# Retention and two dense layers on one core: retention units from the fifth on taken in pairs, the carried-state products in column halves

## The chip, the cores and the metric

The kernel runs on one core of a Trainium2 chip, as one program. The metric is the device time of an execution in microseconds. The engines are named as the profile names them: PE is TensorE (matmuls; its weight loads are listed as PEld), DVE is VectorE, ACT is ScalarE, POOL is GpSimd, SP is SyncE, which here issues nearly all transfers.

## What is computed

Retention over 2 batches, 8 heads, 768 tokens and a head dimension of 64, and after it two dense layers (512 to 1536, gated, back to 512; then 512 to 2048, leaky, back to 512). The change lies wholly in the retention.

```python
for t in range(S):
    state = gamma[None, :, None, None] * state + np.einsum('bhd,bhe->bhde', k[:, :, t], v[:, :, t])
    y[:, :, t] = scale * np.einsum('bhd,bhde->bhe', q[:, :, t], state)
...
a = x @ w_a
b = x @ w_b
return (a * b @ w_out).astype(np.float32)
...
g = np.maximum(0.01 * h, h)
return (g @ w_out).astype(np.float32)
```

## The kernel before

The 1536 tokens are three tiles of 512 (`t`), the 8 heads four pairs (`p`). A **unit** is one tile of one pair; there are 12, numbered 0 to 11, tile by tile. A unit's 512 tokens are four chunks of 128. The recurrence is rewritten by chunks: what a token gets from its own chunk is a masked product of scores, and what it gets from earlier chunks comes through a carried state of 64x64 for each head.

For each unit there are four loads of 256 KB (`q`, `k`, `n`, `v`: the queries and keys with the head dimension on the partitions, the keys and values with the tokens there), and then:

- `prep`: ACT scales `n` into `kd` in two instructions, and POOL scales `q` into `qs` (DVE does it for units 0 and 1).
- `scores`: PE multiplies `k` by `qs`, eight matmuls, for each head on its own 64 rows of the array; DVE scales and masks the two results into `P` (two instructions).
- `states`: PE multiplies `kd` by `v`, six or eight matmuls, each on 64 columns of the array; DVE runs the carried state along (`cr`, three or four short instructions).
- `spreads`: ACT copies the states into `wk`, a 128x128 matrix for each chunk, which has one head's state in each of two opposite corners and zeros elsewhere (four copies in units 4 to 7, two in the others).
- `within`: PE multiplies `v` by `P`, eight matmuls on 64 columns each, into a PSUM bank `xp`.
- `across`: PE adds `wk` times `qs` to the same bank, one matmul of 128 columns for each chunk that has a predecessor (three in units 0 to 7, four in units 8 to 11). Then `split` writes the result as a rounded part on ACT (`x4h` for unit 4) and the remainder on DVE (`x4l`).

A matmul in full precision shows as two matmul records and two weight loads. PSUM has eight banks, which are used in turn; a unit takes four (two for scores, one each for `kv` and `xp`).

Each engine works off its instructions in the order in which the program emits them. The order is written out by hand in the loop at the end of the attention part: in step `u`, scores and states of unit `u + 1`, then within and across of unit `u`, spreads of `u + 1`, `prep` of `u + 3`. Beside that, from step 3 on, each step takes one piece of preparing the first layer's first weight, `a0`: two ACT operations that take its 64-bit raw form apart (L255, L256), four on DVE (`sign` L270, min L272, shift L274, add L278), and a split into `a0h` (ACT) and `a0l` (DVE). The first matmuls of the first layer (`pa`, lines 215 to 217) use `a0h` twice and then `a0l`. The raw form of `a0`, 512 KB, is loaded ahead of unit 5's four loads.

Of the kernel before, what the change touches and what calls it, by code (L numbers as in the profile page):

```python
# [19 lines left out]
B, H, S, D = 2, 8, 768, 64  # L20
# [5 lines left out]
CPT = TT // P  # L26
# [4 lines left out]
NSLOT = 81  # L31
NRAW = 4
NEXTRA = 10
EARLY = 3
NWARM = 7
COUNT = {"a": FF1, "b": FF1, "wo": FF1, "wi": FF2, "wq": FF2}
HALF = FF2 // 2
# [150 lines left out]
def retention_moe_kernel(ctx: ExitStack, tc: tile.TileContext, ins, out):  # L188
    nc = tc.nc
# [46 lines left out]
    def load_weights():  # L236
        if at["load"] < len(order) and at["load"] < at["round"] + NRAW:
            kind, f = order[at["load"]]
            src, i = source[kind]
            t = rawp.tile([P, TT], I64, tag="raw", name=f"raw_{kind}{f}")  # L240
            nc.sync.dma_start(t, src[f, i])
            raws[kind, f] = t
            at["load"] += 1
# [128 lines left out]
    consts, chain, spread = [], [], []  # L372

    def attention_constants():
        for p in range(NPAIR):
            consts.append(ap.tile([P, P], F32, tag=f"cst{p}", name=f"cst{p}"))

        for p in range(NPAIR):
            chain.append([ap.tile([P, CPT, D], F32, tag=f"cr{p}{j}", name=f"cr{p}{j}") for j in range(2)])

        for i in range(2):
            spread.append(ap.tile([P, CPT, P], F32, tag=f"wk{i}", name=f"wk{i}"))
            nc.gpsimd.memset(spread[i][0:D, :, D:P], 0.0)
            nc.gpsimd.memset(spread[i][D:P, :, 0:D], 0.0)

    units = [(t, p) for t in range(NTILE) for p in range(NPAIR)]
    un = {}
# [95 lines left out]
    def spreads(u):  # L483

        if u >= len(units):
            return
        t, p = units[u]
        chunks = [t * CPT + j for j in range(CPT)]
        own = chain[p][t % 2]
        used = [c % CPB != 0 for c in chunks] + [False]  # L490
        runs = [(a, used.index(False, a)) for a in range(CPT) if used[a] and not (a and used[a - 1])]
        for a, b in runs:
            for h in range(2):
                r = slice(h * D, (h + 1) * D)
                nc.scalar.copy(spread[u % 2][r, a:b, h * D:(h + 1) * D], own[r, a:b])
        un[u]["S"] = spread[u % 2]

    cols = [slice(j * P, (j + 1) * P) for j in range(CPT)]

# [14 lines left out]
    def across(u):  # L514
        t, p = units[u]
        d = un.pop(u)
        xp = d["x"]
        later = [(t * CPT + j) % CPB != 0 for j in range(CPT)]
        for j, c in enumerate(cols):
            if later[j]:  # L520
                nc.tensor.matmul(xp[:, c], d["S"][:, j], d["qs"][:, c], start=False, stop=j == CPT - 1)  # L521
        x[t, p] = split(xp, f"x{u}")
        slots.done(4)


    h = {}
# [83 lines left out]
    for _ in range(NWARM):  # L610
        nc.tensor.matmul(wps, warm[:, 0:P], warm, start=True, stop=True)
    for u in range(1, 7):
        if u == 5:
            load_weights()
        loads(u)
    prep(0)
    def first_weights():
# [5 lines left out]

    micro = first_weights()
    prep(1)
    for u in range(-1, len(units)):
        scores(u + 1)
        slots.tick()
        if u == 0:
            within(u)  # L630
        states(u + 1)
        slots.tick()
        if u >= EARLY:
            next(micro, None)
        if u + 1 == len(units) - 1:
            spreads(u + 1)
        if u > 0:
            within(u)
        if u >= 0:
            across(u)  # L640
        if u + 1 < len(units) - 1:
            spreads(u + 1)
        if u < 0:
            prep(2)
        else:
            prep(u + 3)
        loads(u + 8)
        if u + 8 >= len(units) - 1:
            load_weights()
        slots.tick()  # L650
    att.close()
# [79 lines left out]
    for n in range(FF1 - 1, len(z.plan) - 2):  # L731
# [6 lines left out]
        name, j = z.plan[n]  # L738
# [109 lines left out]
    for n in range(FF2 - 1, len(z.plan) - 2):  # L848
# [7 lines left out]
        name, j = z.plan[n]  # L856
# [71 lines left out]
```

## Time and profile before

| | |
|---|---|
| runs | 588.07, 588.76, 588.95 us; median 588.76 us |
| span of the profiled execution, first to last instruction | 587.1 us |
| its own time | not told apart from the runs; the median lies 1.7 us above its span |
| PE busy | 578.6 us, 99% of the span |
| DVE busy | 452.5 us, 77% |
| ACT busy | 308.5 us, 53% |
| attention part | from the first scores at 6.31 us to the first matmul of the first layer at 50.27 us |

The page's shares are over the whole span. In the first twelfth of it, where the change is, the engines stand differently, so views of that stretch are used: the timeline (each instruction's start and length, merged where like ones follow each other), the windows (busy time in stretches) and the chain of waits. The idle time that a row of the timeline gives in brackets is the time in which the engine did nothing just before, and what ended it.

### The profile page before, as it was taken

What the parts mean: (1) busy time and instruction counts of PE and PEld (TensorE: products, weight loads), DVE (VectorE), ACT (ScalarE), POOL (GpSimd) and SP (SyncE); (2) the same over time, 40 slices, a digit from 0 to 9 for tenths busy, and PEclk for the clock granted to TensorE, in tenths of its full rate; (3) what the DMA queues carried; (4) which work ended last, traced back from release to release, by engine and by line L of the source; (5) the groups of instructions that cost most, each with busy time, mean ns of one, the idle gap of its engine ahead of it and who ended that gap; (6) DMA issues with size and microseconds to landing.
All of it is one profiled execution on the core that took longest, in us unless ns stands there. A gap on an engine that the chain in (4) does not pass through costs nothing.

```text
span 587.1 us, 8742 instructions
## 1 busy us (share of the span) xinstructions
PE 578.6 (99%) x3247; PEld 488.8 (83%) x3247; DVE 452.5 (77%) x937; ACT 308.5 (53%) x656; POOL 22.0 (4%) x32
## 2 busy tenths in 40 slices
PE   7999999999999999999999999999999999999997
PEld 5788788888888888888888888888888888888886
DVE  4795688889877788889999938657775766879992
ACT  4674446455354344547657356554633356788710
POOL 2430000000000000000000000000000000000000
PEclk9999999999999999999999999999999999999999
DMA  8991244555433343340014102213220000010111
GB/s 306 361 387 47 88 139 151 178 180 179 162 106 124 98 156 116 118 158 22 1 54 143 56 3 105 97 48 107 73 71 2 2 0 1 0 56 1 54 55 54
DMA packets 23050, 59.62 MB, mean 102 GB/s; under 512 B 2784, under 2 KB 4448, under 8 KB 23008
## 3 DMA queue, kind: packets, MB, share of 16 engines
q1 hardware_dynamic: 21600, 55.13, 28.0%
q0 software_dynamic: 1120, 3.67, 1.6%
q8 instruction: 25, 0.41, 0.3%
q10 hardware_dynamic: 288, 0.27, 0.1%
q14 instruction: 17, 0.14, 0.1%
HBM read 52.24 MB, written 6.82 MB: 101 GB/s over the span
## 4 chain that ended last, share of the span: by engine, by line
PE 91%; DMA 4%; DVE 3%; ACT 1%; issue 0%; SPq 0%; DVEq 0%
PE blk L216 11%; PE blk L215 11%; PE blk L217 11%; PE h L215 7%; PE h L216 7%; PE h L217 7%; PE pa L215 5%; PE pa L216 5%; PE pa L217 5%; PE pb L217 5%; PE pb L216 5%; PE pb L215 5%; DMA v<-in_vn 2%; PE xp L521 1%; DMA n<-in_kn 1%; PE sc L437 1%
## 5 line engine op out<-in xcount | busy, mean ns | idle before, releaser
L216 PE MATMUL blk<-form,form 128*128 128x512 f32 (+1 forms) x224 | 75.7, 338 | 0.0
L215 PE MATMUL blk<-form,form 128*128 128x512 f32 (+1 forms) x224 | 75.5, 337 | 0.0
L217 PE MATMUL blk<-form,form 128*128 128x512 f32 (+1 forms) x224 | 75.3, 336 | 0.0
L543 ACT COPY h<-pa 128x512 f32<-128x512 f32 x33 | 19.5, 590 | 84.6 <-PE pa L217 84.6
L779 ACT ACTIVATE g<-h 128x512 f32<-128x512 f32 x48 | 28.6, 597 | 62.2 <-PE h L217 62.2
L138 DVE TENSOR_TENSOR form<-g,form 128x512 fp32r<-128x512 f32 x112 | 57.3, 553 | 2.4 <-ACT form L132 0.7
L216 PE MATMUL blk<-forma,forma 128*128 128x512 f32 (+1 forms) x168 | 57.0, 339 | 0.4 <-DVE forma L138 0.4
L132 ACT CAST form<-g 128x512 fp32r<-128x512 f32 x112 | 52.6, 514 | 8.4 <-DVE g L113 6.4
L215 PE MATMUL blk<-forma,forma 128*128 128x512 f32 (+1 forms) x168 | 56.6, 337 | 0.0
L217 PE MATMUL blk<-forma,forma 128*128 128x512 f32 (+1 forms) x168 | 56.5, 336 | 0.0
L138 DVE TENSOR_TENSOR form<-wq,form 128x256 fp32r<-128x256 f32 x56 | 23.6, 421 | 35.5 <-ACT form L132 35.4
L215 PEld LDWEIGHTS blk<-form,form 128*128 128x128 f32 x224 | 42.5, 190 | 5.5
L216 PEld LDWEIGHTS blk<-form,form 128*128 128x128 f32 x224 | 42.5, 190 | 5.0
L217 PEld LDWEIGHTS blk<-form,form 128*128 128x128 f32 x224 | 42.3, 189 | 4.7
L138 DVE TENSOR_TENSOR forma<-h,forma 128x512 fp32r<-128x512 f32 x84 | 43.1, 553 | 0.8
L132 ACT CAST forma<-h 128x512 fp32r<-128x512 f32 x84 | 38.8, 511 | 0.0
L216 PEld LDWEIGHTS blk<-forma,forma 128*128 128x128 f32 x168 | 31.8, 189 | 4.6 <-DVE forma L138 0.9
L215 PEld LDWEIGHTS blk<-forma,forma 128*128 128x128 f32 x168 | 31.8, 190 | 4.1
L217 PEld LDWEIGHTS blk<-forma,forma 128*128 128x128 f32 x168 | 31.7, 189 | 3.5
L113 DVE TENSOR_TENSOR g<-g,g 128x512 f32<-128x512 f32 (+1 forms) x56 | 30.7, 571 | 3.6 <-ACT g L779 3.6
L546 DVE TENSOR_TENSOR h<-h,pb 128x512 f32<-128x512 f32 x33 | 22.5, 683 | 8.4 <-PE pb L217 5.4
L132 ACT CAST forma<-wo 128x256 fp32r<-128x256 f32 x42 | 17.1, 407 | 17.4 <-PE blk L217 13.2
(3091 smaller groups left out, 1447.3 us busy)
## 6 DMA issues: line engine op xcount, KB each, us to landing
raw_wi<-in_w SPq DMA_DIRECT2D x16, 512.0 KB, 3.2
raw_wq<-in_w SPq DMA_DIRECT2D x16, 512.0 KB, 3.4
raw_a<-in_wab SPq DMA_DIRECT2D x12, 512.0 KB, 3.2
raw_b<-in_wab SPq DMA_DIRECT2D x12, 512.0 KB, 3.4
raw_wo<-in_wo SPq DMA_DIRECT2D x12, 512.0 KB, 3.3
q<-in_qT SPq DMA_DIRECT2D x12, 256.0 KB, 5.2
n<-in_kn SPq DMA_DIRECT2D x12, 256.0 KB, 5.2
v<-in_vn SPq DMA_DIRECT2D x12, 256.0 KB, 5.3
```

What stands on the lines that cost most here:

```text
L113: queue.append((cost, lambda piece=piece: run(*(self.A(*x[1:], j)[piece] for x in (d, x0, x1)))))
L132: nc.scalar.copy(h, src)
L138: nc.vector.tensor_sub(*todo.pop(0))
L215: nc.tensor.matmul(ps, w[0], x[0], start=first, stop=False, skip_group_check=more)
L216: nc.tensor.matmul(ps, w[0], x[1], start=False, stop=False, skip_group_check=more)
L217: nc.tensor.matmul(ps, w[1], x[0], start=False, stop=last, skip_group_check=more)
L437: nc.tensor.matmul(sc[h][:, c], d["k"][r, c], d["qs"][r, c], start=True, stop=True)
L521: nc.tensor.matmul(xp[:, c], d["S"][:, j], d["qs"][:, c], start=False, stop=j == CPT - 1)
L543: nc.scalar.copy(h[t, f], pa)
L546: nc.vector.tensor_mul(h[t, f], h[t, f], pb)
L779: nc.scalar.activation(g[t, f], ps, AF.Lrelu, alpha=0.01)
```

## The change

Units 0 to 3 keep their steps. From unit 4 on, two units make a group, and in each step a kind of work is done for both before the next kind: scores of both, states of both, within of both units of the group before, across of both. Further:

- In `across` each matmul of 128 columns becomes two of 64 columns, one for each head, which write to the two halves of the bank's partitions.
- `prep` of the next two units is emitted ahead of `across` (where the coming group is a pair), and so its `kd` stands ahead of the `x..h` of `split` in ACT's order.
- `spreads` of both units of a group follow each other; there are four `wk` matrices instead of two, so POOL clears two more at the start. In the last group they stand ahead of `across`, as before.
- The pieces of preparing `a0` come two at a time at the end of a step, first after the group of units 4 and 5, last after the group of units 8 and 9.
- The raw form of `a0` is loaded between unit 9's and unit 10's loads.

```diff
--- before.py
+++ after.py
@@ -31,7 +31,7 @@
 NSLOT = 81
 NRAW = 4
 NEXTRA = 10
-EARLY = 3
+SINGLE = 4
 NWARM = 7
 COUNT = {"a": FF1, "b": FF1, "wo": FF1, "wi": FF2, "wq": FF2}
 HALF = FF2 // 2
@@ -378,7 +378,7 @@
         for p in range(NPAIR):
             chain.append([ap.tile([P, CPT, D], F32, tag=f"cr{p}{j}", name=f"cr{p}{j}") for j in range(2)])
 
-        for i in range(2):
+        for i in range(4):
             spread.append(ap.tile([P, CPT, P], F32, tag=f"wk{i}", name=f"wk{i}"))
             nc.gpsimd.memset(spread[i][0:D, :, D:P], 0.0)
             nc.gpsimd.memset(spread[i][D:P, :, 0:D], 0.0)
@@ -492,8 +492,8 @@
         for a, b in runs:
             for h in range(2):
                 r = slice(h * D, (h + 1) * D)
-                nc.scalar.copy(spread[u % 2][r, a:b, h * D:(h + 1) * D], own[r, a:b])
-        un[u]["S"] = spread[u % 2]
+                nc.scalar.copy(spread[u % 4][r, a:b, h * D:(h + 1) * D], own[r, a:b])
+        un[u]["S"] = spread[u % 4]
 
     cols = [slice(j * P, (j + 1) * P) for j in range(CPT)]
 
@@ -518,7 +518,11 @@
         later = [(t * CPT + j) % CPB != 0 for j in range(CPT)]
         for j, c in enumerate(cols):
             if later[j]:
-                nc.tensor.matmul(xp[:, c], d["S"][:, j], d["qs"][:, c], start=False, stop=j == CPT - 1)
+                for h in range(2):
+                    r = slice(h * D, (h + 1) * D)
+                    nc.tensor.matmul(
+                        xp[r, c], d["S"][:, j, r], d["qs"][:, c], start=False, stop=j == CPT - 1
+                    )
         x[t, p] = split(xp, f"x{u}")
         slots.done(4)
 
@@ -610,8 +614,6 @@
     for _ in range(NWARM):
         nc.tensor.matmul(wps, warm[:, 0:P], warm, start=True, stop=True)
     for u in range(1, 7):
-        if u == 5:
-            load_weights()
         loads(u)
     prep(0)
     def first_weights():
@@ -623,29 +625,46 @@
 
     micro = first_weights()
     prep(1)
-    for u in range(-1, len(units)):
-        scores(u + 1)
+    groups = [[u] for u in range(SINGLE)] + [[u, u + 1] for u in range(SINGLE, len(units), 2)]
+    prepared = 2
+    for n in range(-1, len(groups)):
+        now = groups[n] if n >= 0 else []
+        then = groups[n + 1] if n + 1 < len(groups) else []
+        for u in then:
+            scores(u)
         slots.tick()
-        if u == 0:
-            within(u)
-        states(u + 1)
+        if n == 0:
+            within(0)
+        for u in then:
+            states(u)
         slots.tick()
-        if u >= EARLY:
+        if n > 0:
+            for u in now:
+                within(u)
+        last = n + 2 == len(groups)
+        if last:
+            for u in then:
+                spreads(u)
+        if len(then) == 2:
+            while prepared <= then[-1] + 2:
+                prep(prepared)
+                prepared += 1
+        for u in now:
+            across(u)
+        if not last:
+            for u in then:
+                spreads(u)
+        while prepared <= (then or now)[-1] + 2:
+            prep(prepared)
+            prepared += 1
+        if now and now[0] >= SINGLE:
             next(micro, None)
-        if u + 1 == len(units) - 1:
-            spreads(u + 1)
-        if u > 0:
-            within(u)
-        if u >= 0:
-            across(u)
-        if u + 1 < len(units) - 1:
-            spreads(u + 1)
-        if u < 0:
-            prep(2)
-        else:
-            prep(u + 3)
-        loads(u + 8)
-        if u + 8 >= len(units) - 1:
+            next(micro, None)
+        for u in now:
+            loads(u + 7)
+            if u == 2:
+                load_weights()
+        if now and now[-1] + 7 >= len(units):
             load_weights()
         slots.tick()
     att.close()
```

**Order on ACT.** The first piece is ACT's order before, from the `kd` of unit 9 on (a number behind a name is the unit; `wk` is followed by the number of its buffer, `cr` by that of the head pair; `x2` stands for two instructions).

```order
L415 ACTIVATE kd9_98_608<-n9_59_333,small_74 128x4x64 x2
L209 CAST x7h_102_652<-xp7_640 128x512
L495 COPY wk0_88<-cr00_80 64x4x64 x2
L415 ACTIVATE kd10_104_658<-n10_69_391,small_74 128x4x64 x2
L209 CAST a0h_108_687<-a0_73_419 128x512
L209 CAST x8h_110_704<-xp8_691 128x512
L495 COPY wk1_91<-cr10_82 64x4x64 x2
L415 ACTIVATE kd11_112_710<-n11_80_452,small_74 128x4x64 x2
L209 CAST x9h_116_752<-xp9_739 128x512
```

The same place on ACT with the change, from the `kd` of unit 10 on.

```order
L415 ACTIVATE kd10_102_681<-n10_79_491,small_74 128x4x64 x2
L415 ACTIVATE kd11_104_686<-n11_96_609,small_74 128x4x64 x2
L209 CAST x6h_106_697<-xp6_663 128x512
L209 CAST x7h_108_707<-xp7_672 128x512
L495 COPY wk0_88<-cr00_80 64x4x64 x2
L495 COPY wk1_91<-cr10_82 64x4x64 x2
L495 COPY wk2_94<-cr20_84 64x4x64 x2
L495 COPY wk3_97<-cr30_86 64x4x64 x2
L209 CAST x8h_114_797<-xp8_767 128x512
L209 CAST x9h_116_809<-xp9_776 128x512
L209 CAST a0h_118_816<-a0_93_599 128x512
```

The `kd` of unit 11 stood behind `x8h`; now it stands ahead of `x6h`. The `a0h` stood ahead of `x8h`, and now stands behind the four spreads of units 8 to 11 and behind `x8h` and `x9h`.

**Order on DVE.** Before, from the add of `a0` (the ISA row) on.

```order
L278 ISA a0_73_419<-a0_73_419,low0_420 128x1024
L210 TENSOR_TENSOR x7l_103_653<-xp7_640,x7h_102_652 128x512
L443 SCALAR_TENSOR_TENSOR P90_106_673<-sc90_663,small_74,causal_75 128x512
L443 SCALAR_TENSOR_TENSOR P91_107_675<-sc91_664,small_74,causal_75 128x512
L478 SCALAR_TENSOR_TENSOR cr10_82<-cr10_82,small_74,kv9_677 128x64 x3
L210 TENSOR_TENSOR a0l_109_688<-a0_73_419,a0h_108_687 128x512
L210 TENSOR_TENSOR x8l_111_705<-xp8_691,x8h_110_704 128x512
```

With the change, from the remainder of unit 6 to that of `a0`.

```order
L210 TENSOR_TENSOR x6l_107_698<-xp6_663,x6h_106_697 128x512
L210 TENSOR_TENSOR x7l_109_708<-xp7_672,x7h_108_707 128x512
L272 TENSOR_SCALAR a0_93_599<-a0_93_599 128x512
L274 SCALAR_TENSOR_TENSOR a0_93_599<-a0_93_599,sign0_603 128x512
L443 SCALAR_TENSOR_TENSOR P100_110_729<-sc100_719,small_74,causal_75 128x512
L443 SCALAR_TENSOR_TENSOR P101_111_731<-sc101_720,small_74,causal_75 128x512
L443 SCALAR_TENSOR_TENSOR P110_112_743<-sc110_733,small_74,causal_75 128x512
L443 SCALAR_TENSOR_TENSOR P111_113_745<-sc111_734,small_74,causal_75 128x512
L478 SCALAR_TENSOR_TENSOR cr20_84<-cr20_84,small_74,kv10_747 128x64 x3
L478 SCALAR_TENSOR_TENSOR cr30_86<-cr30_86,small_74,kv11_757 128x64 x3
L210 TENSOR_TENSOR x8l_115_798<-xp8_767,x8h_114_797 128x512
L210 TENSOR_TENSOR x9l_117_810<-xp9_776,x9h_116_809 128x512
L278 ISA a0_93_599<-a0_93_599,low0_600 128x1024
L210 TENSOR_TENSOR a0l_119_817<-a0_93_599,a0h_118_816 128x512
```

The add of `a0` stood behind the states of unit 8, and now stands behind everything of units 8 to 11 but `x10l` and `x11l`; `a0l` follows it.

## Rows read from the trace of the kernel before

**Rows 1.** The page, busy us of each engine (share of the span) and instructions.

```profile
PE 578.6 (99%) x3247; PEld 488.8 (83%) x3247; DVE 452.5 (77%) x937; ACT 308.5 (53%) x656; POOL 22.0 (4%) x32
```

**Rows 2.** Windows: stretch, us, busy by engine, clock, DMA share, GB/s.

```profile
34.00:37.00 3.00, 3.00 (x49) 2.59 (x48) 2.96 (x8) 2.46 (x7) 0.40 (x2) 1.00 1.06 401
...
120.00:587.00 467.00, 463.57 (x2306) 393.38 (x2305) 362.35 (x754) 243.37 (x519) 5.96 (x11) 1.00 0.23 75
```

**Rows 3.** The chain of waits in order of time: start us, us, what.

```profile
16.13 7.49 DMA n<-in_kn
...
26.72 1.02 PE xp L521 x6
```

**Rows 4.** Timeline of PE: start us, us, engine, line, operation, shapes, count.

```profile
31.00 1.16 PE L437 MATMUL sc<-qs,k 64*128 64x128 f32 x16
...
32.49 1.04 PE L506 MATMUL xp<-P,v 128*64 128x128 f32 x16
33.47 0.94 PE L521 MATMUL xp<-qs,wk 128*128 128x128 f32 x6
34.34 1.16 PE L437 MATMUL sc<-qs,k 64*128 64x128 f32 x16
...
40.13 1.16 PE L521 MATMUL xp<-qs,wk 128*128 128x128 f32 x8
41.22 1.16 PE L437 MATMUL sc<-qs,k 64*128 64x128 f32 x16
...
50.81 0.40 PE L217 MATMUL pa<-x0h,a0l 128*128 128x512 f32 x1
```

**Rows 5.** Groups of 0 to 130 us: within's weight loads, busy us, mean ns, idle.

```profile
L506 PEld LDWEIGHTS xp<-P,v 128*64 128x64 f32 x192 | 10.5, 137 | 0.3
```

**Rows 6.** Timeline of DVE, 27 to 56 us.

```profile
31.76 0.42 DVE L272 TENSOR_SCALAR a<-a 128x512 f32<-128x512 f32 x1
...
34.65 0.68 DVE L274 SCALAR_TENSOR_TENSOR a<-a,sign 128x512 int32<-128x512 int32 x1
35.25 0.68 DVE L210 TENSOR_TENSOR x6l<-xp,x6h 128x512 fp32r<-128x512 f32 x1
35.85 1.40 DVE L443 SCALAR_TENSOR_TENSOR P<-sc,small,causal 128x512 f32<-128x512 f32 x2
37.17 0.90 DVE L478 SCALAR_TENSOR_TENSOR cr<-cr,small,kv 128x64 f32<-128x64 f32 x3
37.99 0.68 DVE L278 CUSTOM_DVE_ANT_0 a<-a,low 128x1024 uint16<-128x1024 uint16 x1
38.59 0.69 DVE L210 TENSOR_TENSOR x7l<-xp,x7h 128x512 fp32r<-128x512 f32 x1
...
41.33 0.69 DVE L210 TENSOR_TENSOR a0l<-a,a0h 128x512 fp32r<-128x512 f32 x1
```

**Rows 7.** Timeline of ACT, 22 to 56 us.

```profile
23.64 0.91 ACT L415 ACTIVATE kd<-n,small 128x256 f32<-128x256 f32 x2 [1.99 <-DMA n<-in_kn]
...
34.92 1.15 ACT L495 COPY wk<-cr 64x128 f32<-64x128 f32 x4
...
39.92 0.60 ACT L209 CAST a0h<-a 128x512 fp32r<-128x512 f32 x1
41.38 0.59 ACT L209 CAST x8h<-xp 128x512 fp32r<-128x512 f32 x1 [0.86 <-PE xp L521]
41.86 0.83 ACT L495 COPY wk<-cr 64x256 f32<-64x256 f32 x2
42.72 0.91 ACT L415 ACTIVATE kd<-n,small 128x256 f32<-128x256 f32 x2
```

**Rows 8.** Timeline of POOL: the scaling of q for units 4, 5, 9, 10, 11.

```profile
18.32 1.27 POOL L419 TENSOR_TENSOR qs<-q,cst 128x512 f32<-128x512 f32 x1 [2.82 <-DMA q<-in_qT]
22.36 1.27 POOL L419 TENSOR_TENSOR qs<-q,cst 128x512 f32<-128x512 f32 x1 [2.76 <-DMA q<-in_qT]
...
32.95 1.28 POOL L419 TENSOR_TENSOR qs<-q,cst 128x512 f32<-128x512 f32 x1 [1.39 <-DMA q<-in_qT]
36.83 1.28 POOL L419 TENSOR_TENSOR qs<-q,cst 128x512 f32<-128x512 f32 x1 [2.60 <-DMA q<-in_qT]
39.47 1.28 POOL L419 TENSOR_TENSOR qs<-q,cst 128x512 f32<-128x512 f32 x1 [1.35 <-PE kv L466]
```

## Prediction

> **What bounds the kernel now.** I read the page first: TensorE is busy 99% of the span [rows 1], and from 120 us on it is busy 463.6 of 467 us [rows 2]. So whatever delays or advances the first matmul of the first layer arrives at the end undiminished, and the question is only when that matmul can run. I then read the windows and timelines of the attention part. There the reader is to see three things that are all close to full. TensorE is busy 3.00 of 3.00 us between 34 and 37 us, but VectorE is at 2.96 [rows 2], and the transfers bring a unit (four loads) every 2.65 us: the scaling of q starts at 22.36 us for unit 5 and at 32.95 for unit 9, so 10.6 us for four [rows 8]. TensorE needs 3.33 us for a unit (31.00 to 34.34 [rows 4]). The chain of waits says the same in order of time: up to 26.7 us it runs through loads (a load of n is 7.49 us of it), after that through TensorE [rows 3]. So TensorE has only some 0.4 to 0.6 us in 3.3 to win before VectorE or the loads take over.
>
> **What the change takes off TensorE.** Eight matmul records of `across` go from 40.13 to the next scores at 41.22, 1.09 us; six go from 33.47 to 34.34, 0.87 [rows 4]. A matmul is two records, so a record costs 0.11, six should cost 0.66, and 0.21 is over. A unit in all: scores 8 x 0.11 (two rows of heads side by side), states 6 x 0.055, within 8 x 0.11, across 0.66, sum 2.75, against 3.33 measured. The 0.58 that is over falls on three changes between shapes (64 rows, 64 columns, whole array), 0.19 each. With column halves `across` has the shape of `within`, so one change goes in each of 12 units: 2.3 us. Pairs remove one of two others for every second unit, eight in four pairs: 1.5 us. One change appears, before the first layer: 0.2. Sum 3.6 us less work for TensorE. The halves themselves cost nothing if two heads' halves run side by side as those of `within` do: its 16 records take 0.98 us [rows 4].
>
> Here a rule speaks against the change. The row first: within's 192 loads of 64 columns last 137 ns each, 26.3 us added up, but together occupy 10.5 us with 0.3 us of idle before them [rows 5], so loads and matmuls of that very shape overlap. The Trainium skill, page "TensorE: Matmul & The Clock Gate", Part 3, states that a weight load overlaps matmuls in flight only when their row group differs, which two column halves over all 128 rows do not fulfil. By that sentence across would grow; by the row it does not. I take the row, and give the rule's mechanism as the last rival.
>
> **What the loads do.** The raw weight stood ahead of unit 5's loads: between units 4 and 5 lie 4.04 us (18.32 to 22.36) where 2.65 is usual [rows 8], so it costs 1.4. Units 5 to 9 now land 1.4 us sooner. Units 10 and 11 gain nothing, since the raw weight now stands ahead of them: q of unit 11 lands by 39.5 as before [rows 8], and its n two loads later, at 39.4 + 2 x 0.66 = 40.7. Issuing each unit's loads a step later, and SyncE's shorter path to units 5 to 9, change nothing else: SyncE is that far ahead. The two further clears on GpSimd run before its first operand lands. The two further `wk` buffers cost nothing.
>
> **What the pairs add: waits in ACT's order.** This is the term that decides. The `kd` of both coming units now stand ahead of the rounding of the finished units. So `x3h` waits for n of unit 7, `x4h` for n of unit 9, `x6h` for n of unit 11, and VectorE waits behind these. Before, `kd11` stood two units later, and nobody waited for it (it ran at 42.72, with no idle before it [rows 7]).
>
> I work the timetable out from row lengths, as distances from one start to the next. VectorE: `P` of a unit 1.32, states 0.82, `x..l` 0.60, shift 0.60, add 0.60, min 0.4 [rows 6]. ACT: `kd` 0.9, `x..h` 0.48, spreads 0.86, `a0h` 0.6 [rows 7]; 0.15 for handing over.
>
> TensorE first. Scores 5 now follow scores 4 directly; `qs5` is there at 22.36 - 1.4 + 1.28 = 22.3, while scores 4 end at 18.32 + 1.27 + 1.1 = 20.7: it stands 1.6. Scores 7 (q at 26.3, ready at 27.5) stand some 0.9, within 6 up to 0.9, because its bank is freed by `x4l`, which waits through `x4h` and `kd9` for n of unit 9 (32.9 to 34.1). Then `x6h`:
>
> - n of unit 11 lands at 40.7; `kd11` until 41.5, `x6h` until 42.0, VectorE starts `x6l` at 42.1. It was free by 41.5 even in the late case (34.1 + 0.9 + 0.48 + 0.15 = 35.6, then two remainders, sign, two `P` and two states, 1.2 + 0.5 + 2.64 + 1.64 = 6.0).
> - VectorE: `x6l`, `x7l` 1.2, min and shift 1.0, `P` of 10 and 11 2.64, states 1.64, sum 6.5: 48.6.
> - ACT: the spreads of unit 10 overlap the last states; those of unit 11 from 48.7 to 49.6, `x8h` until 50.05. TensorE gets `across` of 10 and 11 after its spreads, 48.7 + 2 x 0.9 = 50.5, about where it ended before in spite of 3.6 us less work.
> - VectorE: `x8l`, `x9l` 50.2 to 51.4, add 52.0; ACT `a0h` 52.1 to 52.75; `a0l` at 52.8, done at 53.4.
>
> Before, `a0l` ran at 41.33 [rows 6], nine microseconds ahead of need. The matmul that reads it ran at 50.81 [rows 4]; now it can't before 53.4. That is 2.6 us later. The next weights follow `x11l` on VectorE, which moves by about as much, so the distance between TensorE and VectorE is as before, and no later wait changes. The sum: the profiled execution has a span of 587.1 and the runs' median is 1.7 above it; span 589.7, time 588.76 + 2.6 = 591.4 us.
>
> Bounds of the sum. Handing over between engines is not in one row: 0.1 or 0.2 each, on about ten steps, gives half a microsecond either way. The price of a change between shapes doesn't enter, since TensorE waits at the end. A load held up: q of unit 10 came 3.88 us after unit 9's, not 2.65 [rows 8]; if that hold falls away the chain gains at most 0.6, as VectorE is busy until 41.5 otherwise. So 590.4 to 592.4 for this case.
>
> **Rivals.**
>
> *TensorE stays the bound* and the 3.6 us arrive: 585.2. For it: TensorE is continuously busy from 26.7 us on [rows 2, 3]. Against it: VectorE has 0.04 us in 3 left [rows 2]. It decides where n of units 7, 9 and 11 stands: this case needs each of them landed and scaled by the time that TensorE ends `across` of the group before (about 25.7, 32.5 and 39.3), and by the rows they land at 27.6, 32.9 to 34.1, and 40.7. Two would have to come over a microsecond sooner, without the raw weight being moved further. 9%.
>
> *The loads come sooner than reckoned*: with the raw weight out of the stream, the units behind it land more than 1.4 us earlier and unit 11 some 1.2 to 2 us earlier; then the whole timetable from scores 7 on moves by that much, less what VectorE can't follow, and 0.6 to 1.2 us of loss remain: about 589.7, no change that can be seen. For it: the interval before unit 10 holds 1.2 us that isn't bytes. Against it: what lies ahead of unit 11 in the queue is the same. 14%.
>
> *A second hold falls on units 10 and 11*: as the one of 1.2 us, added to the timetable: 592.6. 5%.
>
> *The halves don't run side by side*, so the change doesn't do what it says: each pair of halves then pays a load of 0.137 [rows 5] that nothing hides, 6 x 0.137 in eight units, 8 x 0.137 in four, 11 us; waits of some 5 us in the stage take up part, and 6 come on top of my sum: 597. That is what the skill's rule above would make of it. The row of the same shape speaks against it. 2%.
>
> **How the numbers follow.** My case has 70%. Slower by over 0.2% (1.2 us, about what a measurement of this kernel can tell from no change) are it, the second hold and the last rival: 0.77. Within it is the case of sooner loads: 0.14. Faster is TensorE as the bound: 0.09. My case and the second hold are 75%, so the range must reach down into the sooner loads: 589.0 to 592.8.
>
> **What would show it.** Right: in the timeline of ACT, `kd` of units 7, 9 and 11 with idle before them that a load of n ended, and `x3h`, `x4h`, `x6h` straight behind; TensorE idle some 1.6 us before the second scores of units 4 and 5; at the end of the attention part about 2 us of TensorE idle, ended by `a0h` or `a0l`; across as twelve records of 64 columns, two starting side by side, with 0.2 us less per unit, and TensorE's work in the stage shorter although the stage is longer. Wrong: if ACT never waits for n ahead of an `x..h`; if `a0l` runs before TensorE is through with across of unit 11; or if the delay at the first matmul of the first layer isn't found again at the end, because a later stage had slack.

## The result, and the profile after

The changed kernel took 591.80, 590.75, 591.70 and 591.97 us, median 591.75, beside 588.66 us for the kernel before on the same chip: ratio 1.0051, 95% interval 1.0037 to 1.0066, so 3 us slower. The profiled execution (591.80 us) has a span of 589.9 us against 587.1. The forecast was 591.4, slower. That it came so close is luck: two errors of 1.7 us each cancel, so the steps matter here more than the sum.

The busy times hardly differ from [rows 1], as the change only reorders. The page after:

```profile
PE 578.1 (98%) x3327; PEld 489.1 (83%) x3327; DVE 452.4 (77%) x937; ACT 308.3 (52%) x656; POOL 23.2 (4%) x36
```

The timeline of PE after, which answers to [rows 4]: start, length, shapes, records, and in brackets the idle time before and what ended it.

```profile
21.39 1.16 PE L437 MATMUL sc<-qs,k 64*128 64x128 f32 x16 [1.14 <-POOL qs L419]
...
26.79 1.16 PE L437 MATMUL sc<-qs,k 64*128 64x128 f32 x16 [0.77 <-POOL qs L419]
...
28.63 1.92 PE L506 MATMUL xp<-P,v 128*64 128x128 f32 x32
30.38 1.48 PE L523 MATMUL xp<-qs,wk 128*64 128x128 f32 x24
...
34.52 1.92 PE L506 MATMUL xp<-P,v 128*64 128x128 f32 x32
...
46.78 2.38 PE L523 MATMUL xp<-qs,wk 128*64 128x128 f32 x32
51.24 0.50 PE L215 MATMUL pa<-x0h,a0h 128*128 128x512 f32 x1 [2.08 <-ACT a0h L209]
51.58 0.39 PE L216 MATMUL pa<-x0l,a0h 128*128 128x512 f32 x1
51.97 0.79 PE L217 MATMUL pa<-x0h,a0l 128*128 128x512 f32 x1
52.56 0.63 PE L215 MATMUL pa<-x1h,a0h 128*128 128x512 f32 x1
52.99 0.63 PE L216 MATMUL pa<-x1l,a0h 128*128 128x512 f32 x1
...
61.38 0.39 PE L215 MATMUL pb<-x0h,b0h 128*128 128x512 f32 x1
```

The same matmuls of the first layer in the kernel before, and the first that uses the second matrix (`pb`):

```profile
51.05 0.40 PE L215 MATMUL pa<-x1h,a0h 128*128 128x512 f32 x1
51.28 0.39 PE L216 MATMUL pa<-x1l,a0h 128*128 128x512 f32 x1
...
58.56 0.39 PE L215 MATMUL pb<-x0h,b0h 128*128 128x512 f32 x1
```

Three things are to be seen. A pair goes round in 34.52 - 28.63 = 5.89 us, where two units took 2 x 3.33 = 6.66: the saving of work is there. TensorE then stands 1.14, 0.77 and, at the end, 2.08 us. And the two matmuls of `x1` start 0.43 us apart, where they go 0.23 apart in the kernel before.

The timeline of ACT after ([rows 7] before): `kd` of units 7, 9 and 11, each followed at once by an `x..h`.

```profile
26.78 0.91 ACT L415 ACTIVATE kd<-n,small 128x256 f32<-128x256 f32 x2 [1.79 <-DMA n<-in_kn]
27.59 0.56 ACT L209 CAST x3h<-xp 128x512 fp32r<-128x512 f32 x1
...
32.18 0.91 ACT L415 ACTIVATE kd<-n,small 128x256 f32<-128x256 f32 x2 [0.86 <-DMA n<-in_kn]
32.99 0.56 ACT L209 CAST x4h<-xp 128x512 fp32r<-128x512 f32 x1
...
39.02 0.91 ACT L415 ACTIVATE kd<-n,small 128x256 f32<-128x256 f32 x2 [0.66 <-DMA n<-in_kn]
39.83 0.56 ACT L209 CAST x6h<-xp 128x512 fp32r<-128x512 f32 x1
...
46.32 1.69 ACT L495 COPY wk<-cr 64x256 f32<-64x256 f32 x4 [3.86 <-DVE cr L478]
48.03 0.59 ACT L209 CAST x8h<-xp 128x512 fp32r<-128x512 f32 x1
...
50.57 0.62 ACT L209 CAST a0h<-a 128x512 fp32r<-128x512 f32 x1 [1.47 <-DVE a L278]
```

The timeline of DVE after ([rows 6] before), at the remainders and the last pieces of `a0`.

```profile
40.43 0.69 DVE L210 TENSOR_TENSOR x6l<-xp,x6h 128x512 fp32r<-128x512 f32 x1 [0.93 <-DMA raw_a<-in_wab]
...
48.65 0.69 DVE L210 TENSOR_TENSOR x8l<-xp,x8h 128x512 fp32r<-128x512 f32 x1 [1.59 <-ACT x8h L209]
49.26 0.68 DVE L210 TENSOR_TENSOR x9l<-xp,x9h 128x512 fp32r<-128x512 f32 x1
49.86 0.68 DVE L278 CUSTOM_DVE_ANT_0 a<-a,low 128x1024 uint16<-128x1024 uint16 x1
51.22 0.69 DVE L210 TENSOR_TENSOR a0l<-a,a0h 128x512 fp32r<-128x512 f32 x1 [0.68 <-ACT a0h L209]
```

ACT and VectorE together read as one chain: `n` of unit 11, `kd11`, `x6h`, `x6l` (with `x7l` and two pieces of `a0` behind it), the `P` and states of units 10 and 11, their spreads, `x8h`, `x8l`, `x9l`, the add, `a0h`, `a0l`, and then TensorE. (The row of `x6l` names the raw weight as what ended its wait; `x6h` ended right before it, at 40.39, and that is the wait that closes: the pieces that read the raw weight, L270, L255 and L256, had run.) `a0l` ran nine microseconds ahead of need before; now TensorE waits for it.

The timeline of POOL after, for units 4, 5, 9, 10 and 11 ([rows 8] before).

```profile
17.33 1.28 POOL L419 TENSOR_TENSOR qs<-q,cst 128x512 f32<-128x512 f32 x1 [1.88 <-DMA q<-in_qT]
20.06 1.27 POOL L419 TENSOR_TENSOR qs<-q,cst 128x512 f32<-128x512 f32 x1 [1.45 <-DMA q<-in_qT]
...
30.95 1.28 POOL L419 TENSOR_TENSOR qs<-q,cst 128x512 f32<-128x512 f32 x1 [1.40 <-DMA q<-in_qT]
35.08 1.29 POOL L419 TENSOR_TENSOR qs<-q,cst 128x512 f32<-128x512 f32 x1 [2.85 <-DMA q<-in_qT]
37.75 1.27 POOL L419 TENSOR_TENSOR qs<-q,cst 128x512 f32<-128x512 f32 x1 [1.39 <-PE xp L523]
```

Unit 5 follows unit 4 by 2.73 us instead of 4.04. Unit 10 follows unit 9 by 4.13 us with the raw weight between them, and by 3.88 before without it. So unit 11 comes at 37.75, 1.7 us sooner than before, where I had expected no gain.

The windows after, over the first matmuls of the first layer. Columns: stretch, us, busy us of each engine, granted clock of TensorE, DMA share, GB/s.

```profile
51.00:53.00 2.00, 1.76 (x5) 1.14 (x6) 1.78 (x3) 2.00 (x5) 0.00 (x0) 0.74 0.00 0
53.00:55.00 2.00, 2.00 (x6) 1.61 (x5) 1.83 (x5) 0.32 (x1) 0.00 (x0) 0.50 0.26 45
55.00:57.00 2.00, 2.00 (x9) 1.61 (x9) 1.03 (x2) 1.49 (x3) 0.00 (x0) 0.91 0.54 217
57.00:59.00 2.00, 2.00 (x11) 1.65 (x10) 0.00 (x0) 0.83 (x2) 0.00 (x0) 1.00 0.00 0
```

In the kernel before the clock is 1.00 in all four; one of them:

```profile
53.00:55.00 2.00, 2.00 (x11) 1.65 (x10) 1.12 (x3) 0.82 (x2) 0.00 (x0) 1.00 0.71 256
```

After the change it is at half (1.2 instead of 2.4 GHz) for about three microseconds, from about 52.0 to 55.4 us. It falls some 0.7 us after TensorE has taken up work again at 51.24, not in the wait itself. From the first `pa` matmul that reads `a0l` to the first of `pb` it is 7.75 us before (50.81 to 58.56) and 9.41 after (51.97 to 61.38).

**Where the time went.** The first matmul that reads `a0l` starts 51.97 - 50.81 = 1.16 us later, and the stretch behind it is 9.41 - 7.75 = 1.66 us longer. Together that is 2.82 us, the whole difference of the spans.

### The profile page after: what moved, and what is told of

It is laid out like the page before. It is cut to its first block, busy times and chain, and to the rows that moved or that the text cites. A ratio compares the mean times of both kernels' runs of the same rounds, so it can differ in the third digit from the quotient of the medians.

```text
span 589.9 us, 8901 instructions
## 1 busy us (share of the span) xinstructions
PE 578.1 (98%) x3327; PEld 489.1 (83%) x3327; DVE 452.4 (77%) x937; ACT 308.3 (52%) x656; POOL 23.2 (4%) x36
## 4 chain that ended last, share of the span: by engine, by line
PE 89%; DMA 6%; DVE 3%; ACT 1%; SPq 0%; issue 0%; DVEq 0%; ACTq 0%
PE blk L216 11%; PE blk L215 11%; PE blk L217 11%; PE h L215 7%; PE h L216 7%; PE h L217 7%; PE pa L217 6%; PE pa L215 6%; PE pa L216 6%; PE pb L217 5%; PE pb L215 5%; PE pb L216 5%; DMA n<-in_kn 3%; DMA v<-in_vn 2%; DMA k<-in_kT 1%; DMA raw_a<-in_wab 1%
## 5 line engine op out<-in xcount | busy, mean ns | idle before, releaser
L217 PE MATMUL blk<-form,form 128*128 128x512 f32 (+1 forms) x224 | 75.3, 336 | 0.0
L217 PE MATMUL blk<-forma,forma 128*128 128x512 f32 (+1 forms) x168 | 56.4, 336 | 0.0
L217 PEld LDWEIGHTS blk<-form,form 128*128 128x128 f32 x224 | 42.3, 189 | 4.7
L217 PEld LDWEIGHTS blk<-forma,forma 128*128 128x128 f32 x168 | 31.7, 189 | 3.5
```

What stands on the lines that cost most here:

```text
L217: nc.tensor.matmul(ps, w[1], x[0], start=False, stop=last, skip_group_check=more)
```

## Experiments

The theory: what costs time is not the pairs or the halves, but where two things came to stand with them, `kd` of the second coming unit ahead of `x..h`, and `a0` behind `x8h`, `x8l`, `x9l`; and TensorE's standing before the first layer, which is followed by half its clock. The rivals: the halves cost time; the pairs cost time; the move of the raw weight does; or the clock has nothing to do with it. "kernel before" is the one in the same job (588.66 us in that of the change; 588.66 for c1 to c4, 588.47 for c5 to c8, 588.56 for c9 to c11). L217 is the start of the first `pa` matmul that reads `a0l` (50.81 before, 51.97 after), in the profiled execution.

| run | median us (lowest to highest, executions) | ratio to before, 95% interval | L217 |
|---|---|---|---|
| the change | 591.75 (590.75 to 591.97, 4) | 1.0051, 1.0037 to 1.0066 | 51.97 |
| c1_halves_alone | 588.11 (587.40 to 588.84, 11) | 0.9991, 0.9982 to 0.9999 | 49.18 |
| c2_pairs_alone | 591.90 (590.59 to 592.92, 6) | 1.0057, 1.0044 to 1.0069 | 52.33 |
| c3_a0_ahead | 588.76 (587.69 to 590.56, 12) | 1.0002, 0.9993 to 1.0011 | 51.24 |
| c4_filler | 590.78 (590.46 to 591.95, 5) | 1.0040, 1.0028 to 1.0052 | 52.21 |
| c5_kd_a0 | 587.17 (586.52 to 588.05, 11) | 0.9977, 0.9969 to 0.9986 | 49.21 |
| c6_kd_between | 590.10 (588.51 to 591.62, 11) | 1.0028, 1.0015 to 1.0041 | 51.83 |
| c7_no_halves | 592.44 (591.15 to 592.78, 5) | 1.0062, 1.0048 to 1.0076 | 51.93 |
| c8_raw_early | 592.42 (591.85 to 593.92, 5) | 1.0068, 1.0055 to 1.0082 | 52.60 |
| c9_best_whole | 587.86 (587.22 to 588.16, 11) | 0.9987, 0.9978 to 0.9996 | 49.16 |
| c10_best_raw_early | 588.63 (588.12 to 589.64, 11) | 1.0002, 0.9993 to 1.0010 | 50.48 |
| c11_kd_between_filler | 589.09 (588.58 to 590.15, 11) | 1.0008, 0.9999 to 1.0017 | 51.86 |

**The halves alone** (c1_halves_alone): the kernel before with

```diff
-                nc.tensor.matmul(xp[:, c], d["S"][:, j], d["qs"][:, c], start=False, stop=j == CPT - 1)
+                for h in range(2):
+                    r = slice(h * D, (h + 1) * D)
+                    nc.tensor.matmul(
+                        xp[r, c], d["S"][:, j, r], d["qs"][:, c], start=False, stop=j == CPT - 1
+                    )
```

> The kernel before, with the products of across in column halves and nothing else. The theory: each unit loses the change of shape between within and across, 0.1 to 0.2 us of TensorE's work, and TensorE, which sets the end of the attention part in the kernel before, can use a part of it until VectorE and the loads stop it: the first matmul of the first layer that reads the rounding remainder (50.81 us before) comes about 1 us sooner, time about 587.7. across of eight units in 12 pairs takes about 0.75 us instead of 0.87. Rival, the halves cost TensorE time because their weight loads are not hidden: across takes over 1.5 us and the time is 5 us or more above the kernel before. Rival, VectorE and the loads leave nothing: no change, 588.7.

Measured 588.11, 0.5 us below the kernel before; the interval only just leaves out no change. The timeline of PE of its profiled execution, across of unit 11 and the first matmul that reads `a0l`:

```profile
47.17 1.51 PE L523 MATMUL xp<-qs,wk 128*64 128x128 f32 x16 [0.22 <-ACT wk L495]
...
49.18 0.40 PE L217 MATMUL pa<-x0h,a0l 128*128 128x512 f32 x1
```

That execution, 587.55 us, is among the lowest of the eleven; in it TensorE waits for a spread, so VectorE and ACT stop it, as expected. The halves cost nothing, and gain about half of what I expected. The rival that they cost time falls.

**The pairs alone** (c2_pairs_alone): the changed kernel with `across` as it was and the raw weight ahead of unit 5's loads again.

```diff
-                for h in range(2):
-                    r = slice(h * D, (h + 1) * D)
-                    nc.tensor.matmul(
-                        xp[r, c], d["S"][:, j, r], d["qs"][:, c], start=False, stop=j == CPT - 1
-                    )
+                nc.tensor.matmul(xp[:, c], d["S"][:, j], d["qs"][:, c], start=False, stop=j == CPT - 1)
...
     for u in range(1, 7):
+        if u == 5:
+            load_weights()
         loads(u)
...
             loads(u + 7)
-            if u == 2:
-                load_weights()
```

> The changed kernel with across in whole matmuls of 128 columns and the raw weight ahead of unit 5's loads again: of the change only the pairs are left. The theory: the roundings x3h, x4h and x6h stand behind kd of units 7, 9 and 11 on ACT and wait for n, the remainder a0l is late by 1.4 to 3.3 us against need, and TensorE stands waiting for it before the first layer, which gives it half its clock for some microseconds: first matmul of the first layer that reads the remainder at 52.2 to 54.1 us, and up to 1.7 us more from the clock: 590.2 to 593.5. Rival, what costs time in the change is the move of the raw weight: 588.7 or less. Rival, TensorE's work decides: pairs alone take away 1.5 us of it, 587.2.

Measured 591.90: as slow as the whole change, with neither of the other two parts in it. L217 is at 52.33, TensorE stands 1.15 us before the first layer, and its clock there stays at 1.00; it fell in this execution from 23 to 27 us instead, behind a wait of 1.62 us for `qs5`:

```profile
22.46 1.72 PE L437 MATMUL sc<-qs,k 64*128 64x128 f32 x16 [1.62 <-POOL qs L419]
```

From there no row of TensorE has idle time until the 1.15 us, which `a0h` ends, so the slow matmuls used up time in which it would have stood. The profiled execution, 590.59 us, is the lowest of the six; what makes the others up to 2.3 us longer, no trace shows. So the pairs in this order are the part that costs time. Whether it is the pairs as such or the places of `kd` and `a0` is what the next runs ask.

**a0 ahead** (c3_a0_ahead): in the changed kernel, the last two pieces of `a0` ahead of the `across` of units 8 and 9.

```diff
         if last:
             for u in then:
                 spreads(u)
+            next(micro, None)
+            next(micro, None)
...
-        if now and now[0] >= SINGLE:
+        if now and now[0] >= SINGLE and not last:
```

> The changed kernel with one thing moved: the last two pieces of a0 (the sum on VectorE, a0h on ACT and a0l on VectorE) ahead of the across of the pair 8 and 9 and so ahead of x8h, x8l and x9l. The theory: the chain to a0l loses x8h and two remainders, some 1.7 to 2.2 us, and a0l is done about when TensorE is through with across of the last pair; so TensorE doesn't stand before the first layer, keeps clock 1.00 there, and the first matmul that reads a0l starts at about 49.2 to 50 us instead of 51.97: 587.2 to 588.0. If only the waiting counts and the clock doesn't matter: 589.5. Rival, the pairs and halves as such cost time in the attention part, wherever a0 stands: 591.7, as the changed kernel.

Measured 588.76, 3.0 us below the changed kernel, 0.8 above the upper end of what I expected. The timeline of ACT of its profiled execution:

```profile
40.59 0.91 ACT L415 ACTIVATE kd<-n,small 128x256 f32<-128x256 f32 x2 [0.48 <-DMA n<-in_kn]
...
49.60 0.62 ACT L209 CAST a0h<-a 128x512 fp32r<-128x512 f32 x1
```

Here `n` of unit 11 landed 1.57 us later than in the changed kernel (`kd11` 40.59 against 39.02), in a load order that is the same. Taken from that landing, L217 comes after 51.24 - 40.59 = 10.65 us instead of 51.97 - 39.02 = 12.95: 2.3 us are gained, and TensorE doesn't stand before the first layer (clock 1.00 in all windows). So the place of `a0` is most of the loss; and the landing of the loads moves between executions by more than I had allowed. That may be why this kernel's executions lie 2.9 us apart; only one of them has a trace.

**Filler** (c4_filler): eight matmuls in TensorE's wait.

```diff
+    fill = bank("fill")
+    for _ in range(8):
+        nc.tensor.matmul(fill, warm[:, 0:P], warm, start=True, stop=True)
     att.close()
```

> The changed kernel with eight matmuls of 128x512 into a spare bank, whose results nobody reads, in the stretch in which TensorE waits for a0: work that is no part of the computation. The wait itself stays. The theory that TensorE's clock falls because it stood idle there (2.08 us, then 0.50 of the clock from 53 to 55 us): clock 1.00 in all windows from 51 to 59 us, the stretch from the first matmul that reads a0l to the first of the second matrix shrinks from 9.41 to about 7.8 us, time about 590.1. Rival, the longer stretch comes from the order of the work or from a late weight and not from the clock: 591.7. Rival, the filler itself is in the way: 592 or more.

The timeline of PE of its profiled execution, and a row of its windows:

```profile
49.34 1.90 PE L672 MATMUL fill<-warm 128*128 128x512 bf16 x8
51.48 0.50 PE L215 MATMUL pa<-x0h,a0h 128*128 128x512 f32 x1 [0.24 <-ACT a0h L209]
...
52.21 0.50 PE L217 MATMUL pa<-x0h,a0l 128*128 128x512 f32 x1
...
60.05 0.39 PE L215 MATMUL pb<-x0h,b0h 128*128 128x512 f32 x1
```

```profile
53.00:55.00 2.00, 2.00 (x10) 1.66 (x9) 1.83 (x5) 0.52 (x1) 0.00 (x0) 1.00 0.14 20
```

L217 is 0.24 later than in the changed kernel, as `kd11` is (39.26 against 39.02), and the stretch to `pb` is 60.05 - 52.21 = 7.84 us instead of 9.41, at clock 1.00: 1.57 us gained by work that nobody reads. Of the median only 1.0 us shows (590.78 against 591.75), and the two intervals overlap: two of the four executions of the changed kernel have a mean clock of 1.000 and so can have lost little there (one of them took 591.97 us all the same, and has no trace). The trace settles the mechanism, the medians don't.

**kd and a0** (c5_kd_a0): c3_a0_ahead, and `kd` of the second coming unit behind `across`.

```diff
-        if len(then) == 2:
-            while prepared <= then[-1] + 2:
-                prep(prepared)
-                prepared += 1
+        if len(then) == 2 and prepared <= then[-1] + 2:
+            prep(prepared)
+            prepared += 1
         for u in now:
             across(u)
+        if len(then) == 2 and prepared <= then[-1] + 2:
+            prep(prepared)
+            prepared += 1
```

> The run with a0 ahead of x8h, and besides kd of the second coming unit behind the across of the finished pair, so that x3h, x4h and x6h wait for n of units 6, 8 and 10 and no longer for n of units 7, 9 and 11. The theory: what costs time in the changed kernel is where kd and a0 stand on ACT and VectorE and nothing in the pairs or halves themselves; with both moved TensorE ends its last across and starts the first layer without a wait: the first matmul that reads a0l starts at 48.2 to 49.5 us by when n of unit 11 lands, time 586 to 587.4, below the kernel before and the halves alone. Rival, the loads of units 10 and 11 set the end whatever the order on ACT: as the run with a0 ahead, 588.8. Rival, kd of the second unit behind x3h, x4h and x6h is late for TensorE's states: 589 or more.

Measured 587.17 us, ratio 0.9977 (0.9969 to 0.9986): below the kernel before, and lower than the halves alone (0.9991, 0.9982 to 0.9999), though these two intervals still touch. The timeline of PE of its profiled execution:

```profile
27.63 1.16 PE L437 MATMUL sc<-qs,k 64*128 64x128 f32 x16 [0.71 <-POOL qs L419]
...
46.79 1.92 PE L523 MATMUL xp<-qs,wk 128*64 128x128 f32 x32
48.64 0.50 PE L215 MATMUL pa<-x0h,a0h 128*128 128x512 f32 x1
...
49.21 0.39 PE L217 MATMUL pa<-x0h,a0l 128*128 128x512 f32 x1
```

Behind 27.63 us no row has an idle time any more (one wait of some 0.3 us, for `qs11`, lies within the scores of units 10 and 11: 2.34 us where the pair before took 2.06). This run has the pairs, the halves and the late raw weight, all three, and differs from the changed kernel only in where `kd` and `a0` stand; it is 4.6 us below it (4.4 by the two ratios). So the three together don't cost time once `kd` and `a0` stand elsewhere.

**kd alone** (c6_kd_between): the `kd` part of the diff above, with `a0` left where the change put it.

> The changed kernel with kd of the second coming unit behind the across of the finished pair and a0 where it is. The theory: x6h, P and the spreads of units 10 and 11 come about 1.4 us sooner against the landing of n of unit 11 than in the changed kernel; but TensorE comes sooner too, a0l stays behind x8h, x8l and x9l, and TensorE still stands 2 to 3 us before the first layer, with its clock at half for some time: 590 to 591. Were a0's place of no account, the time would be that of the run with both moved, 586 to 587.4; were kd's place of no account, that of the changed kernel, 591.7.

Measured 590.10, so `a0`'s place alone costs 2.9 us against c5_kd_a0. With the changed kernel, c3_a0_ahead and c5_kd_a0 this makes a square, and the two parts add up in it: moving `a0` gives 3.0 us with `kd` where the change put it and 2.9 with `kd` moved; moving `kd` gives 1.65 and 1.6. The eleven executions fall into two sets by TensorE's mean granted clock: five at 0.996 or 0.997 with 591.14 to 591.62 us, six at 0.999 or 1.000 with 588.51 to 590.10. The profiled one is of the second set: TensorE stands 1.42 us, and its clock stays at 1.00. So the median, the highest of the lower set, stands between two cases.

**No halves** (c7_no_halves): the changed kernel with the first hunk of c2_pairs_alone.

> The changed kernel with across in whole matmuls of 128 columns: pairs and the late raw weight stay. The theory: in the changed kernel what the halves save, 0.1 to 0.2 us a unit, goes into TensorE's waits, since VectorE and ACT set the time of a0l: no change, 591 to 592.2, with across 0.1 to 0.2 us a unit longer and the wait before the first layer shorter by what is saved behind the last wait for a spread. Since that wait is shorter, the clock may stay up, which gives at most 1.7 us back: down to 590. Rival, TensorE's work decides: 593 or more, a loss of some 2 us in 12 units.

Measured 592.44, 0.2 above the range I gave, with an interval that overlaps the changed kernel's: no difference that can be told. Across of a pair takes longer, a pair goes round in 34.82 - 28.70 = 6.12 us instead of 5.89, and L217 starts at 51.93 instead of 51.97. I had thought that the clock might stay up with a shorter wait. It didn't: TensorE stood 1.98 us and the clock was 0.50 from 53 to 55 us.

**Raw weight early** (c8_raw_early): the changed kernel with the second hunk of c2_pairs_alone.

> The changed kernel with the raw weight ahead of unit 5's loads again: pairs and halves stay. The theory: what counts is the landing of n of unit 11, ahead of which the raw weight stands in both places, so the place of the raw weight moves the time by no more than the landing of that n moves between executions, some 1 us: 591 to 593. Units 5 to 9 land 1.2 to 1.5 us later than in the changed kernel. Rival, the late raw weight is what saves or costs time: 590 or less, or 594 or more.

Measured 592.42, as expected: 0.7 above the changed kernel, with overlapping intervals. `qs5` starts at 21.56 instead of 20.06, `qs11` at 37.79 instead of 37.75. So the move of the raw weight isn't what costs time.

**c5_kd_a0 with whole products** (c9_best_whole, the first hunk of c2_pairs_alone on c5_kd_a0):

> The run with kd and a0 moved, with across in whole matmuls of 128 columns. The theory: where TensorE sets the end, the halves are worth what their shape saves, 0.22 us in each pair of the runs before (5.89 against 6.11 us a pair with and without them): behind the last wait for a q three and a half pairs are left, so 0.7 to 1.0 us are lost, 587.9 to 588.2, where the same edit in the changed kernel lost nothing that was certain. Rival, the loads or VectorE set the end here too: no change, 587.2.

Measured 587.86, 0.7 above c5_kd_a0: where TensorE sets the end, the halves are worth something. The intervals against before overlap (0.9978 to 0.9996 and 0.9969 to 0.9986), so the size is uncertain; that it is work and not a wait, the trace shows: a pair goes round in 34.93 - 28.81 = 6.12 us, with no idle time, and from its last wait for a `q` to L217 TensorE takes 49.16 - 26.97 = 22.19 us, where c5_kd_a0 takes 49.21 - 27.63 = 21.58. L217 itself stands at the same place in these two executions, since the loads came 0.7 us sooner in this one (`qs5` at 20.23 against 20.96).

**c5_kd_a0 with the raw weight early** (c10_best_raw_early, the second hunk of c2_pairs_alone on c5_kd_a0):

> The run with kd and a0 moved, with the raw weight ahead of unit 5's loads again. The theory: TensorE's last waits are those for q of units 5 and 7, which land 1.2 to 1.5 us later with the raw weight ahead of them, and from there on TensorE never waits: the whole loss arrives at the end, 588.3 to 588.7. Rival, n of unit 11 and VectorE set the end, ahead of which the raw weight stands in either place: no change, 587.2.

Measured 588.63, 1.5 above c5_kd_a0. Two rows of its windows show that the way there was not quite the one expected:

```profile
24.00:26.00 2.00, 2.00 (x38) 1.88 (x36) 1.60 (x4) 0.23 (x2) 1.28 (x1) 0.64 1.05 374
26.00:28.00 2.00, 2.00 (x24) 2.00 (x22) 1.01 (x5) 0.77 (x2) 0.75 (x1) 0.50 1.05 391
```

TensorE stood 2.57 us for `qs5`, got half its clock until about 28 us, and by then `qs7` was there: the wait for it that was expected went into slow matmuls. All eleven executions but one have a mean clock of 0.997 or less. The sum is the one expected: behind 23.20 us TensorE never waits, and its first `pa` matmul starts 49.91 - 48.64 = 1.27 us later.

**kd alone, with filler** (c11_kd_between_filler, c6_kd_between with the filler of c4_filler):

> The run with kd of the second unit moved and a0 where it was, with eight matmuls of 128x512 into a spare bank before the first layer, work that is no part of the computation. Without them five of eleven executions had a mean granted clock of 0.996 or 0.997 and took 591.1 to 591.6 us, six had 0.999 or 1.000 and took 588.5 to 590.1. The theory that the clock falls because TensorE stood idle there: no execution under 0.999, all from 588.5 to 590.3, median about 589.3. Rival, the mean clock only goes along with late loads, which are the cause: two sets of times as without them, median 590.1.

Measured 589.09, 1.0 below c6_kd_between, and the upper set is gone: the highest of eleven is 590.15, where five of eleven lay above 591.1. The mean clock is 0.999 or 1.000 in ten; one has 0.997 and 589.21 us, against what I expected, perhaps from a fall earlier in the stage as in c2_pairs_alone; it has no trace. In the profiled execution L217 starts at 51.86, as without the filler (51.83). So, as far as eleven executions of each can tell, late loads are not the cause of the upper set; TensorE's standing is.

## Why the prediction was right, and where it was wrong

**TensorE's work: right for a pair.** I put a change between shapes at 0.19 us and four of them off two units in pairs with halves, 0.76; measured 6.66 - 5.89 = 0.77. Over the whole stage the sum was too large: PE's busy time from the first scores to the first `pa` matmul falls from 42.30 us (6.31 to 50.27) to 39.89 (6.31 to 51.24), and to 39.28 in c5_kd_a0, so by 2.4 and 3.0 us where I summed 3.6. That the halves' loads overlap, as those of `within` do, holds too. The group of weight loads of `across` after, with busy time, mean ns of one, and idle before; and a window with two `within` and two `across` in it, both of that shape:

```profile
L523 PEld LDWEIGHTS xp<-qs,wk 128*64 128x64 f32 x160 | 9.2, 137 | 0.6 <-ACT wk L495 0.6
```

```profile
45.00:49.00 4.00, 3.85 (x62) 3.30 (x58) 2.27 (x8) 2.58 (x6) 0.00 (x0) 1.00 0.00 0
```

160 loads of 137 ns would be 21.9 us one after the other, and occupy 9.2; across of a unit of six products takes 24.86 - 24.10 = 0.76 us. In the window matmuls fill 3.85 of 4 us and loads 3.30, so the loads run beside matmuls. The rule weighed against the change, a sentence of the Trainium skill's page "TensorE: Matmul & The Clock Gate", Part 3, by which only loads for another row group overlap, taken by itself doesn't hold for these two column halves over all rows.

**The waits in ACT's order: right.** `x3h`, `x4h` and `x6h` each stand right behind a `kd` that waits for `n`. From the start of `kd11` to L217 I worked out 53.4 - 40.7 = 12.7 us; measured 12.95. TensorE's waits ahead of scores 5 and 7 were put at 1.6 and 0.9, measured 1.14 and 0.77. The wait of up to 0.9 us ahead of `within` of unit 6 didn't come, since `n` of unit 9 landed by 32.2 us.

**The loads: wrong by 1.7 us.** The step that failed is "Units 10 and 11 gain nothing": `kd11` started at 39.02, not 40.7. I took the hold of 1.2 us before unit 10 [rows 8] for a property of the queue, and it is one of that execution: from unit 9 to unit 10 c1, c2, c8 and c10 took 2.65 to 2.79 us. The start of `qs11`, with the raw weight ahead of unit 5, is 39.47 before, and 37.63, 37.73, 37.79 and 38.00 in c1, c2, c8 and c10; with the raw weight ahead of unit 10 it is 37.75 after, and from 37.80 to 39.36 in the seven others. c1 issues the same loads in the same order as the kernel before, and is 1.84 us sooner, 0.67 of it at unit 9 already (32.28 against 32.95), the rest by that hold. The bound that I set on it, "at most 0.6, as VectorE is busy until 41.5 otherwise", failed with it: it let unit 11 come early but kept unit 9 late. But unit 9's `kd` ran at 32.18 already, and VectorE was through with the states of units 8 and 9 at 39.5. So on the chain the rival of sooner loads came true, 1.16 us where it said 0.6 to 1.2.

**The clock: missing.** The sum held no term for it; the first `pa` matmuls were taken at the pace of before. Half the clock cost 1.66 us in the profiled execution, and 2.59 - 1.68 + 0.25 (the chain's own error) + 1.66 is the 2.82 measured. That the delay at the first matmul arrives undiminished at the end was right, and so was that TensorE would stand "about 2 us": I forecast the standing and did not ask what follows it. That the stretch is longer because of the clock, and the clock lower because TensorE stood, c4_filler shows.

**What the gain became.** The work that TensorE was spared went into its waits, 1.14 + 0.77 + 0.23 (for `qs11`) + 2.08 us, and with the last of them it came to the first layer later than before. With `kd` and `a0` moved (c5_kd_a0) the rival "TensorE stays the bound" is what happens, at 587.2 rather than 585.2: two waits for loads, 1.30 and 0.71 us ahead of scores 5 and 7, remain. So the grouping pays together with the late raw weight (0.9977, and 0.9987 without the halves); two places in the hand-written order took it back. With the raw weight early it doesn't: c10_best_raw_early is at 1.0002, the halves alone at 0.9991. What the late raw weight is worth without the pairs, no run shows.

Open: what makes the loads hold, and why the clock fell behind some waits and not behind others (below).

## What to carry to other kernels

When work is grouped kind by kind, look at what each in-order queue now has ahead of the things that release others: here one `kd` ahead of the roundings, and two roundings with their remainders ahead of the last pieces of the next stage's weight, cost 4.6 us against the same grouping with these moved. Before a sum rests on when a transfer lands, look at more than one execution, or carry the scatter as a bound: here it was 1.8 us, more than the whole measured effect on the chain (1.16). And where TensorE will stand before a dense stage, put a term for its clock into the sum, as a bound: here up to 1.7 us, in some executions nothing.

## What the runs showed of the hardware that was not expected

TensorE's granted clock fell to half behind short waits, for about 3 us each time, and the matmuls that followed paid for it: 0.43 us apart instead of 0.23. By the windows it fell 0.4 to 1.7 us after TensorE had taken up work again. It fell after waits of 2.08 us (after and c8_raw_early), 1.98 (c7_no_halves), 2.57 (c10_best_raw_early) and 1.62 (c2_pairs_alone, before scores 5); it did not after 2.44 (c8_raw_early, before scores 5), 1.62 (c6_kd_between, before scores 7), 1.42 (c6_kd_between, before the first layer) and 1.15 (c2_pairs_alone). The wait in c6_kd_between is as long as that in c2_pairs_alone:

```profile
28.39 1.16 PE L437 MATMUL sc<-qs,k 64*128 64x128 f32 x16 [1.62 <-POOL qs L419]
```

So the length of the last wait alone doesn't decide it. In the same kernel some executions lost it and some did not, by their mean clocks (five of eleven in c6_kd_between).

What a fall cost at the end depended on what came behind it: in c2_pairs_alone the one at 23 to 27 us was followed by a further wait, which became shorter; in the changed kernel the one at 52 us arrived whole.

The same loads in the same order brought unit 11's `q` at 37.6 in one execution and at 39.5 in another, with 2.7 us from unit 9 to unit 10 in the one and 3.9 in the other.
